# Token mixing gets the urgent rank, and the stacked keys' exponentials take the row maximum as ScalarE's bias

## The chip, the cores and the metric

One Trainium2 chip, one of its cores. The metric is the device time of one execution in microseconds; the median of three runs is given.

## The reference, cut to what matters

Two parts run one after the other: linear attention over 8 batches of 8 heads (576 tokens, 64 columns a head), and a mixer on its result.

```python
def phi(x):                                   # of queries and of keys
    proj = einsum('bhsd,df->bhsf', x, w_phi)  # 64 -> 128 features
    proj = proj - max(abs(proj), axis=-1, keepdims=True)
    return concatenate([exp(proj), exp(-proj)], axis=-1)
kv = einsum('bhsf,bhsd->bhfd', phi(k), v);  z = sum(phi(k), axis=2)
x = einsum('bhsf,bhfd->bhsd', phi(q), kv) / (einsum('bhsf,bhf->bhs', phi(q), z) + 1e-6)
x = x as (8, 576, 512)
h = relu(x^T @ w_tok1) @ w_tok2               # token mixing, 576 -> 256 -> 576
u = x + h^T
out = u + relu(u @ w_ch1) @ w_ch2             # channel mixing, 512 -> 1536 -> 512
```

Note the second exponential: it is exp(-(p - m)), that is exp(-p + m), where m is the largest absolute value of the row.

## The kernel before, in words

Attention works on pairs of heads, numbered i = 0 to 31, four pairs to a batch. `keys()` makes the features of the keys of a pair in five groups of up to two 128-token units and adds them to the pair's `pkv` sum on TensorE (`add_kv`, L326). `queries()` makes the features of the queries, turns them, splits them into a high and a low part (`turn`, L437 to L446) and multiplies them with the finished sum (`numerators`, `pn`); GpSimd's multiplication at L526 writes the attention result of a pair and segment into `xt`. Pairs 0 to 7 (batches 0 and 1) take a plain way; from pair 8 on, keys and queries are "stacked": a high and a low half of the input lie in one tile (`stack`, L215 and L216).

`less_max` is the helper that both share. For stacked inputs it multiplies with the projection (L241), copies one part out of PSUM on ScalarE (`part`, L248), adds on VectorE (`p`, L250, two buffers for keys and queries together), takes the row maximum of the absolute values on VectorE (`mx`, L255), and subtracts it on GpSimd (`pm`, L257). For plain inputs the subtraction runs on VectorE. `keys` then takes two exponentials on ScalarE (L301), one for each sign, over all units of the group.

`token_mix(b, h)` mixes the tokens of one half (two pairs) of batch b: per unit two transposes into `px` (L550), a split on ScalarE and VectorE into `xh` and `xl` (L566, in L77 and L80), matmuls into `pa`; then a ReLU into `ah` and `al` (L575, L576), matmuls into `ph`, and an addition into `xt` (L585). It issues no DMA. From batch 1 on its PSUM tiles `pa`, `px` and `ph` come from the pool REST, five rotating banks that it shares with the projections, `pkv`, `pt` and `pn` of attention. `channel_mix(i)` takes 256 tokens at a time, 18 chunks in all: copies `uh` and `ul`, then six up-projections `h` (24 matmuls each) that alternate with six down-projections `acc` (24 each); `h` has one bank, emptied by ScalarE (`gh`, L616) and VectorE (`gl`, L617). Chunk i starts once the batch of its last token is mixed.

All matmuls written through `mm3` carry line L86, so they are told apart by their tiles.

Two things set the order. `weave` calls the five streams in turn, by shares, and so fixes the order of the program text. Then the framework's planner orders each engine's queue by simulating the kernel: of the instructions that are ready it takes the one with the first rank. The rank is the place in the text, unless the stream is marked urgent (the third entry of its line in L694) and all weights are loaded in the text (L681): then an instruction is ranked as if it stood at the start of the program. Once a queue is ordered, each engine works it off strictly in that order.

Of the kernel before, what the change touches and what calls it, by code (L numbers as in the profile page):

```python
# [12 lines left out]
AF = mybir.ActivationFunctionType  # L13
ALU = mybir.AluOpType
# [5 lines left out]
NP = H // 2  # L20
# [27 lines left out]
def mixer_kernel(ctx, tc, qk, vm, vt, w_phi, w1, w2, wc1, wc2d, out):  # L48
    nc = tc.nc

    cst = ctx.enter_context(tc.tile_pool(name="cst", bufs=1))
    wk = ctx.enter_context(tc.tile_pool(name="wk", bufs=2))
# [17 lines left out]
    def column(pool, n, **kw):  # L70

        return pool.tile([P, 32], F32, **kw)[:, :n]
# [147 lines left out]
    def less_max(ts, units, name, base=None, early=False):  # L220

        n, kind = len(units), name[0]
        if early and base == D:
            ps = ps_a.tile([P, 2, 2, F], F32, tag=f"a{nplain['k'] % 2}", name=f"pp{name}")
            nplain["k"] += 1
        elif early and base == 0 and (nplain["q"] % 2 == 0 or nplain["q"] >= BORROWED):
            ps = ps_h.tile([P, 2, 2, F], F32, tag="h", name=f"pp{name}")
            nplain["q"] += 1  # L230
        elif early and base == 0:
            ps = ps_w.tile([P, 2, 2, F], F32, name=f"pp{name}", **REST)
            nplain["q"] += 1
        elif kind == "k":
            ps = ps_w.tile([P, 2, 2, F], F32, name=f"pp{name}", **REST)
        else:
            ps = ps_w.tile([P, 2, 2, F], F32, name=f"pp{name}", **REST)
        for i, u in enumerate(units):
            t, c = (ts[1], 512) if u is None else (ts[u[0]], P * u[1])
            if base is None:  # L240
                nc.tensor.matmul(ps[:, i].rearrange("p two f -> p (two f)"), t[:, c:c + P],  # L241
                                 wp2.rearrange("p two f -> p (two f)"), start=True, stop=True)
            else:
                rows = slice(D, P) if name == "k0_0" else slice(0, P)
                nc.tensor.matmul(ps[:, i, 0], t[rows, c:c + P], wz[rows, base // D], start=True, stop=True)  # L245
        if base is None:
            part = wk.tile([P, 2, F], F32, tag="part", name=f"part{name}")
            nc.scalar.copy(part[:, :n], ps[:, :n, 1])  # L248
            pr = wk.tile([P, 2, F], F32, tag="p", name=f"p{name}")
            nc.vector.tensor_tensor(pr[:, :n], ps[:, :n, 0], part[:, :n], op=ALU.add)  # L250
            pr, eng = pr[:, :n], nc.gpsimd
        else:
            pr, eng = ps[:, :n, 0], nc.vector
        mx = column(wk, 2, tag=f"mx{kind}", name=f"mx{name}")
        nc.vector.tensor_reduce(mx[:, :n], pr, axis=AX.X, op=ALU.max, apply_absolute_value=True)  # L255
        pm = wk.tile([P, 2, F], F32, tag=f"pm{kind}", name=f"pm{name}", bufs=1 if kind == "t" else 2)
        eng.tensor_tensor(pm[:, :n], pr, mx[:, :n].unsqueeze(2).to_broadcast([P, n, F]), op=ALU.subtract)  # L257
        return pm

    nplain = {"k": 0, "q": 0}  # L260
    raws, pairs, kvs, loaded = {}, {}, {}, set()
# [2 lines left out]
    def load(i):  # L264

        raw = wk.tile([P, 2 * S], F32, tag="raw", name=f"raw{i}", bufs=1)
        lo, hi = (D if i <= PLAIN else 0), (D if i == B * NP else P)
        nc.sync.dma_start(raw[lo:hi], qk[i, lo:hi])
        raws[i] = raw
# [12 lines left out]
    def keys():  # L282
        groups = [[(0, 0), (0, 1)], [(0, 2), (0, 3)], [(1, 0), (1, 1)], [(1, 2), (1, 3)], [None]]
        todo = None
        for i in range(B * NP):
            yield from until(lambda: i < 2 or i - 2 in asked)
            if i < PLAIN:
                load_plain(i)
            else:
                load(i)  # L290
            v_sb, queue = vtiles[i % 2], nc.sync if i else nc.scalar
            queue.dma_start(v_sb[:, 0:4].rearrange("p u j d -> p (u j) d")[:, :, :D], vm[i])
            for j in range(2):
                queue.dma_start(v_sb[j * D:(j + 1) * D, 4, j, :D], vt[i, j])
            plain = D if i < PLAIN else None
            ts = pairs[i] if i < PLAIN else stack(raws[i], D, f"k{i}")
            for g, us in enumerate(groups):
                pm = less_max(ts, us, f"k{i}_{g}", plain, i < NP)
                kp = wk.tile([P, 2, 2, F], F32, tag="kp", name=f"kp{i}_{g}")
                for sg in range(2):  # L300
                    nc.scalar.activation(kp[:, :len(us), sg], pm[:, :len(us)], AF.Exp, scale=1.0 - 2.0 * sg)  # L301
                yield 0.22
                if todo:
                    add_kv(*todo)
                    yield 0.82
                todo = (i, g, us, kp, v_sb)
        add_kv(*todo)
        yield 0.82
# [40 lines left out]
    def queries():  # L349
        waiting, split_up, row_major, pm = [], [], [], None  # L350
        pieces = [(i, k, j) for i in range(B * NP) for k in range(2) for j in range(2)]
        n = 0
        while n < len(pieces) or waiting or split_up or row_major:
            for done in row_major:
                flip(*done)
                yield 0.2
            row_major = []
            for work in split_up:
                yield from until(lambda: work[0] in kvs)
                if work[0] < ROWS:  # L360
                    row_major += [done for done in (row_numerators(*work),) if done]
                else:
                    numerators(*work)
                yield 0.75
            split_up = []
            while waiting and len(split_up) < 2 and (waiting[0][0] <= n or n >= len(pieces)):
                due, work = waiting.pop(0)
                split_up.append(turn(*work, pm if via(work[0]) and n < len(pieces) else None))
                yield 0.02 if via(work[0]) else 0.25
            if n < len(pieces):  # L370
                i, k, j = pieces[n]
                if (k, j) == (0, 0):
                    plain = 0 if i < PLAIN else None
                    if i < PLAIN:
                        yield from until(lambda: i in pairs)
                        ts = pairs[i]
                    else:
                        yield from until(lambda: i + 1 in raws or i + 1 == B * NP)
                        if i + 1 == B * NP:
                            load(i + 1)  # L380
                        ts = stack(raws[i + 1], 0, f"q{i}")
                    asked.add(i)
                    tail = less_max(ts, [None], f"t{i}", plain, i < NP)
                    yield 0.11
                pm = less_max(ts, [(j, 2 * k), (j, 2 * k + 1)], f"q{i}_{k}{j}", plain, i < NP)
                if via(i):
                    across(i, k, j, pm, tail)
                waiting.append((n + 1 + BEHIND * via(i), (i, k, j, pm, tail)))
                yield 0.22
            n += 1  # L390
# [3 lines left out]
    def via(i):  # L394
        return i >= ROWS and i % NP < TURNED
# [134 lines left out]
    def until(cond):  # L530
        while not cond():
            yield None
# [130 lines left out]
    def token_stream():  # L663
        for b in range(B):
            for h in range(2):
                yield from until(lambda: b * NP + 2 * h + 1 in attended and (b > 0 or NP - 1 in kvs))
                yield from token_mix(b, h, xts[b])
            mixed.add(b)
# [6 lines left out]
    def weave(streams):  # L675

        streams = [[g, share, urgent, 0.0] for g, share, urgent in streams]
        now = 0.0
        while streams:
            for s in sorted(streams, key=lambda s: s[3]) * 2:  # L680
                with tc.high_priority() if s[2] and NE - 1 in loaded else nullcontext():  # L681
                    step = next(s[0], "end")
                if step is None:
                    continue
                now = max(now, s[3])
                if step == "end":
                    streams.remove(s)
                else:
                    s[3] = max(s[3], now - LAG) + max(step, 0.01) / s[1]
                break  # L690
            else:
                raise RuntimeError("every stream waits")

    weave([(keys(), 5.2, True), (queries(), 5.2, True), (token_stream(), 8.0, False),  # L694
           (load_weights(), 10.0, False), (channel_stream(), 19.5, False)])


# [40 lines left out]
```

## Time and profile before

| | |
|---|---|
| median of 3 runs | 1117.81 us (1116.67 to 1118.49) |
| the profiled execution | 1116.6 us |
| its span, first to last instruction | 1114.7 us |
| TensorE busy | 1089.5 us, 98%, 9040 matmuls |
| VectorE busy | 721.1 us, 65% |
| GpSimd busy | 571.8 us, 51% |
| ScalarE busy | 560.9 us, 50% |
| mean granted TensorE clock | 0.995 |

The profile is of one execution. A matmul's end in it is modelled, and neighbouring matmuls overlap, so a TensorE that is busy all the time is not one at its peak: the number of matmuls in a stretch, held against a stretch where nothing interferes, says more than the busy share.

### The profile page before, as it was taken

To read this page: it belongs to the slowest core of one execution; us is meant where nothing else is said; L and a number is where in the kernel's file an instruction comes from. 1 tells how busy PE (TensorE), PEld (TensorE's weight loads), DVE (VectorE), ACT (ScalarE), POOL (GpSimd) and SP (SyncE) were. 2 spreads that over 40 slices of the span, in tenths; PEclk is the share of its full clock that TensorE was granted. 3 is DMA by queue.
4 is the path that set the end of the run, shared out by engine and by line. 5 is a ranking of instruction groups with operands and counts; after the bars stand their busy time and mean duration, and the time that the engine had idled before them with its cause. 6 is when DMAs were issued, how large, how long until landed. Compare 5 with 4: busy or idle time off the path is not lost.

```text
span 1114.7 us, 24745 instructions
## 1 busy us (share of the span) xinstructions
PE 1089.5 (98%) x9040; PEld 1074.3 (96%) x9040; DVE 721.1 (65%) x1775; ACT 560.9 (50%) x1589; POOL 571.8 (51%) x1043
## 2 busy tenths in 40 slices
PE   8998999999999899999999999999999999999998
PEld 7898999989999899999999999999999999999998
DVE  6889873557668775867676585774767687642111
ACT  5665542446546565665555464554555666541110
POOL 2235341467648674768667384664666776420110
PEclk9999999999999899999999999999999999999999
DMA  8454411133313332333233132141332323200000
GB/s 215 129 158 146 146 31 52 33 94 76 72 47 94 76 77 77 80 83 81 70 81 68 57 84 72 44 104 41 83 79 55 88 71 64 57 8 19 20 20 20
DMA packets 186746, 82.75 MB, mean 74 GB/s; under 512 B 159424, under 2 KB 171200, under 8 KB 186624
## 3 DMA queue, kind: packets, MB, share of 16 engines
q1 hardware_dynamic: 185104, 80.74, 27.9%
q8 instruction: 72, 1.18, 0.5%
q10 hardware_dynamic: 1520, 0.43, 0.2%
q14 instruction: 50, 0.41, 0.1%
HBM read 57.54 MB, written 23.59 MB: 73 GB/s over the span
## 4 chain that ended last, share of the span: by engine, by line
PE 83%; DVE 6%; POOL 5%; ACT 2%; issue 2%; DMA 2%; SPq 0%; ACTq 0%; POOLq 0%; DVEq 0%
PE h L86 25%; PE acc L86 24%; PE pkv L326 8%; PE pn L86 6%; PE ph L86 4%; PE pa L86 4%; PE pr L471 2%; PE ppk L241 2%; PE ppq L241 2%; POOL stq L216 1%; PE ppk L245 1%; PE px L550 1%; PE ppq L245 1%; POOL pmq L257 1%; PE pt L429 1%
## 5 line engine op out<-in xcount | busy, mean ns | idle before, releaser
L86 PE MATMUL acc<-gh,wc 128*128 128x256 f32 x1728 | 342.1, 284 | 1.8 <-ACT gh L616 1.6
L86 PEld LDWEIGHTS acc<-gh,wc 128*128 128x128 f32 x1728 | 275.4, 188 | 2.8 <-ACT gh L616 2.7
L86 PE MATMUL h<-uh,wc_h 128*128 128x256 f32 x864 | 245.3, 284 | 3.1 <-DVE gl L617 3.0
L86 PE MATMUL h<-uh,wc_l 128*128 128x256 f32 x864 | 244.4, 283 | 0.0
L86 PE MATMUL h<-ul,wc_h 128*128 128x256 f32 x864 | 243.0, 281 | 0.0
L86 PE MATMUL acc<-gl,wc 128*128 128x256 f32 x864 | 242.7, 283 | 0.0
L86 PEld LDWEIGHTS h<-uh,wc_h 128*128 128x128 f32 x864 | 162.7, 188 | 4.4 <-DVE gl L617 3.1
L326 PE MATMUL pkv<-v,kp 128*128 128x65 f32 (+2 forms) x1152 | 164.6, 269 | 1.2 <-ACT kp L301 1.1
L301 ACT ACTIVATE kp<-pmk 128x256 f32<-128x256 f32 (+1 forms) x320 | 109.4, 389 | 108.1 <-POOL pmk L257 82.8
L86 PEld LDWEIGHTS acc<-gl,wc 128*128 128x128 f32 x864 | 162.8, 188 | 0.3 <-DVE gl L617 0.2
L86 PEld LDWEIGHTS h<-ul,wc_h 128*128 128x128 f32 x864 | 162.7, 188 | 0.1
L86 PEld LDWEIGHTS h<-uh,wc_l 128*128 128x128 f32 x864 | 162.5, 188 | 0.1
L326 PEld LDWEIGHTS pkv<-v,kp 128*128 128x128 f32 x1152 | 153.5, 192 | 2.4 <-ACT kp L301 1.8
L617 DVE SCALAR_TENSOR_TENSOR gl<-h,gh 128x512 fp32r<-128x512 f32 x108 | 74.0, 685 | 123.7 <-ACT gh L616 120.7
L616 ACT ACTIVATE gh<-h 128x512 fp32r<-128x512 f32 x108 | 64.3, 596 | 119.4 <-PE h L86 117.8
L446 POOL TENSOR_TENSOR ql<-qf,qh 128x320 fp32r<-128x320 f32 (+1 forms) x96 | 80.1, 835 | 62.4 <-ACT qh L445 58.8
L597 POOL TENSOR_TENSOR ul<-xt,uh 128x64 fp32r<-128x64 f32 (+3 forms) x120 | 61.4, 537 | 87.6 <-ACT uh L596 86.9
L86 PE MATMUL pn<-qh,kv 128*128 128x320 f32 (+1 forms) x384 | 105.2, 304 | 0.9 <-ACT qh L445 0.6
L216 POOL TENSOR_TENSOR stk<-raw,stk 64x512 fp32r<-64x512 f32 (+1 forms) x48 | 68.5, 1428 | 66.6 <-DVE stk L215 45.3
L257 POOL TENSOR_TENSOR pmk<-pk,mxk 128x256 f32<-128x256 f32 (+1 forms) x120 | 71.7, 598 | 57.8 <-DVE mxk L255 56.9
L437 ACT ACTIVATE qf<-qt 128x320 f32<-128x320 f32 (+1 forms) x192 | 81.8, 436 | 37.4 <-POOL qf L436 36.5
L445 ACT ACTIVATE qh<-qt 128x320 fp32r<-128x320 f32 (+1 forms) x192 | 83.0, 437 | 31.4 <-POOL qh L444 25.8
(129 smaller groups left out, 2305.5 us busy)
## 6 DMA issues: line engine op xcount, KB each, us to landing
raw<-in_qk SPq DMA_DIRECT2D x23, 576.0 KB, 3.9
rawc<-in_wc SPq DMA_DIRECT2D x24, 512.0 KB, 4.3
v<-in_vm SPq DMA_DIRECT2D x31, 256.0 KB, 3.9
dq<-tq SPq DMA_DIRECT2D x24, 320.0 KB, 2.1
qt<-dq SPq DMA_DIRECT2D x96, 80.0 KB, 2.8
dq<-tq SPq DMA_DIRECT2D x24, 256.0 KB, 2.0
qt<-dq SPq DMA_DIRECT2D x96, 64.0 KB, 2.8
out_x<-xt SPq DMA_DIRECT2D x12, 256.0 KB, 2.1
```

The costliest lines, as they stand in the source:

```text
L86: nc.tensor.matmul(o, a, m, start=first and i == 0, stop=last and i == 2, skip_group_check=group_ok)
L216: nc.gpsimd.tensor_tensor(t[lo:lo + D], src, t[base:base + D].bitcast(F32), op=ALU.subtract)
L241: nc.tensor.matmul(ps[:, i].rearrange("p two f -> p (two f)"), t[:, c:c + P], wp2.rearrange("p two f -> p (two f)"), start=True, stop=True)
L257: eng.tensor_tensor(pm[:, :n], pr, mx[:, :n].unsqueeze(2).to_broadcast([P, n, F]), op=ALU.subtract)
L301: nc.scalar.activation(kp[:, :len(us), sg], pm[:, :len(us)], AF.Exp, scale=1.0 - 2.0 * sg)
L326: nc.tensor.matmul(o, kp[:, n, sg], v, start=g == 0 and n == 0 and sg == 0, stop=u is None, skip_group_check=True)
L437: nc.scalar.activation(full, src, AF.Exp, scale=1.0 - 2.0 * sg)
L445: nc.scalar.activation(hi, src, AF.Exp, scale=1.0 - 2.0 * sg)
L446: (nc.gpsimd if sg else nc.vector).tensor_tensor(lo, full, hi.bitcast(F32), op=ALU.subtract)
L597: nc.gpsimd.tensor_tensor(l[:, d:d + n], t[:, c, o:o + n], h[:, d:d + n].bitcast(F32), op=ALU.subtract)
L616: nc.scalar.activation(gh, ph, AF.Relu)
L617: nc.vector.scalar_tensor_tensor(gl, ph, 0.0, gh.bitcast(F32), op0=ALU.max, op1=ALU.subtract)
```

## The change

The token stream becomes urgent, like keys and queries. For stacked keys `less_max` no longer subtracts: it negates the maximum on VectorE into a new tile `nmx` (one buffer) and returns the projection with both columns; `keys` then takes each exponential unit by unit, with the negated maximum as bias for the positive sign and the maximum itself for the negative sign. Plain keys, and all queries, stay as they are. No DMA is added or moved in the text.

```diff
+        if base is None and kind == "k":
+            nmx = column(wk, 2, tag="nmx", bufs=1, name=f"nmx{name}")
+            nc.vector.tensor_scalar(nmx[:, :n], mx[:, :n], -1.0, None, op0=ALU.mult)
+            return pr, (nmx, mx)
         pm = wk.tile([P, 2, F], F32, tag=f"pm{kind}", name=f"pm{name}", bufs=1 if kind == "t" else 2)
         eng.tensor_tensor(pm[:, :n], pr, mx[:, :n].unsqueeze(2).to_broadcast([P, n, F]), op=ALU.subtract)
-        return pm
+        return (pm, None) if kind == "k" else pm
...
-                pm = less_max(ts, us, f"k{i}_{g}", plain, i < NP)
+                pm, mx = less_max(ts, us, f"k{i}_{g}", plain, i < NP)
                 kp = wk.tile([P, 2, 2, F], F32, tag="kp", name=f"kp{i}_{g}")
                 for sg in range(2):
-                    nc.scalar.activation(kp[:, :len(us), sg], pm[:, :len(us)], AF.Exp, scale=1.0 - 2.0 * sg)
+                    if mx is None:
+                        nc.scalar.activation(kp[:, :len(us), sg], pm[:, :len(us)], AF.Exp, scale=1.0 - 2.0 * sg)
+                        continue
+                    for u in range(len(us)):
+                        nc.scalar.activation(kp[:, u, sg], pm[:, u], AF.Exp, scale=1.0 - 2.0 * sg,
+                                             bias=mx[sg][:, u:u + 1])
...
-    weave([(keys(), 5.2, True), (queries(), 5.2, True), (token_stream(), 8.0, False),
+    weave([(keys(), 5.2, True), (queries(), 5.2, True), (token_stream(), 8.0, True),
            (load_weights(), 10.0, False), (channel_stream(), 19.5, False)])
```

## Rows read from the trace of the kernel before

**Rows 1.** The page: span, busy time of each engine, and the granted clock.

```profile
span 1114.7 us, 24745 instructions
...
PE 1089.5 (98%) x9040; PEld 1074.3 (96%) x9040; DVE 721.1 (65%) x1775; ACT 560.9 (50%) x1589; POOL 571.8 (51%) x1043
...
PEclk9999999999999899999999999999999999999999
```

**Rows 2.** Busy time by stretch: length, each engine (instructions), granted clock, DMA share, GB/s.

```profile
224.00:252.00 28.00, 25.11 (x201) 24.02 (x200) 17.19 (x43) 13.23 (x41) 18.10 (x34) 1.00 0.37 94
298.00:328.00 30.00, 29.43 (x244) 29.02 (x243) 16.23 (x41) 11.24 (x31) 8.75 (x18) 1.00 0.18 54
358.00:383.00 25.00, 20.54 (x125) 18.03 (x125) 17.31 (x47) 14.82 (x45) 14.98 (x32) 0.86 0.29 79
392.00:420.00 28.00, 28.00 (x239) 28.00 (x239) 20.80 (x52) 18.10 (x54) 20.45 (x41) 1.00 0.35 85
490.00:505.00 15.00, 14.15 (x112) 13.62 (x111) 11.71 (x33) 8.05 (x26) 8.53 (x19) 1.00 0.26 78
890.00:905.00 15.00, 14.17 (x113) 13.65 (x111) 12.01 (x33) 7.92 (x25) 9.08 (x18) 1.00 0.25 79
1036.00:1064.00 28.00, 28.00 (x240) 28.00 (x240) 4.97 (x9) 4.29 (x9) 2.86 (x4) 1.00 0.07 20
```

**Rows 3.** Groups of instructions on TensorE in 358 to 383 us, channel mixing's `h`.

```profile
L86 PE MATMUL h<-uh,wc_l 128*128 128x256 f32 x2 | 0.6, 321 | 0.0
...
L86 PE MATMUL h<-uh,wc_h 128*128 128x256 f32 x1 | 0.3, 281 | 0.0
```

**Rows 4.** Instructions of `pa` alone, by stretch: TensorE, weight loads, VectorE, ScalarE.

```profile
298.00:328.00 30.00, 4.26 (x28) 3.74 (x28) 0.69 (x1) 0.60 (x1) 1.00 0.18 54
...
490.00:505.00 15.00, 4.42 (x28) 3.82 (x28) 0.69 (x1) 0.60 (x1) 1.00 0.26 78
```

**Rows 5.** Instructions in order of time from 296 us, across engines: start, length, engine.

```profile
296.06 0.38 PE L550 MATMUL px<-ident,xt 128*128 128x128 f32 x2
...
299.19 0.28 PE L86 MATMUL pa<-xh,w_h 128*128 128x256 f32 x1
```

**Rows 6.** GpSimd in order of time: two neighbouring multiplications that write attention's result.

```profile
296.77 0.75 POOL L526 TENSOR_TENSOR xt<-xt,den 128x256 f32<-128x256 f32 x1
...
328.21 0.87 POOL L526 TENSOR_TENSOR xt<-xt,den 128x320 f32<-128x320 f32 x1 [1.62 <-DVE den L524]
```

**Rows 7.** TensorE's waits after 160 us: total us, times, longest.

```profile
PE ph L86 <- ACT ah L575: 2.9, 3, 1.5
PE h L86 <- DVE gl L617: 2.2, 3, 1.3
PE pa L560 <- DVE xs L555: 1.9, 2, 1.3
```

**Rows 8.** Groups of instructions by form: count, busy us, mean ns, idle before.

```profile
L301 ACT ACTIVATE kp<-pmk 128x256 f32<-128x256 f32 x256 | 93.3, 411 | 88.2 <-POOL pmk L257 71.1 <-DVE pmk L257 10.2 <-PE pkv L326 4.6
...
L257 POOL TENSOR_TENSOR pmk<-pk,mxk 128x256 f32<-128x256 f32 x96 | 62.0, 645 | 56.2 <-DVE mxk L255 55.9
...
L301 ACT ACTIVATE kp<-pmk 128x128 f32<-128x128 f32 x64 | 16.2, 302 | 19.9 <-POOL pmk L257 11.7 <-DVE pmk L257 4.8 <-PE pkv L326 1.7
...
L485 DVE TENSOR_SCALAR dn<-pr 128x4 f32<-128x4 f32 x16 | 2.5, 154 | 6.0 <-PE pr L471 6.0
```

**Rows 9.** The same view: the two instructions that empty the bank of an up-projection.

```profile
L617 DVE SCALAR_TENSOR_TENSOR gl<-h,gh 128x512 fp32r<-128x512 f32 x108 | 74.0, 685 | 123.7 <-ACT gh L616 120.7 <-POOL wc L80 2.1
...
L616 ACT ACTIVATE gh<-h 128x512 fp32r<-128x512 f32 x108 | 64.3, 596 | 119.4 <-PE h L86 117.8 <-PE acc L86 0.7 <-POOL wc L80 0.2
```

**Rows 10.** ScalarE in order of time, 395 to 411 us: two exponentials back to back, each form.

```profile
395.38 0.49 ACT L301 ACTIVATE kp<-pmk 128x128 f32<-128x128 f32 x2
...
405.20 0.72 ACT L301 ACTIVATE kp<-pmk 128x256 f32<-128x256 f32 x2 [0.21 <-POOL pmk L257]
```

**Rows 11.** Waits of SyncE's DMA queue: total us, times, longest.

```profile
SPq L648 <- DVE xt L647: 187.6, 32, 34.0
```

## The prediction

> **What bounds the kernel now.** I read the page first: TensorE is busy for 1089.5 of 1114.7 us, no other engine for more than 65%, and its clock is granted in full but for one slice of forty [rows 1]. The change neither adds nor removes a matmul, so it can only win or lose where TensorE falls behind its own pace. The second view is the table by stretch, read by number of matmuls. Where channel mixing runs alone, 240 matmuls go through in 28 us, 8.57 per us; the mixed stretch of 392 to 420 us keeps that pace with 239 [rows 2]. Against it four stretches fall behind: 224 to 252 us does 201 matmuls, 23.5 us of work, 4.5 us lost; 358 to 383 us does 125, 14.6 us of work, 10.4 us lost; 490 to 505 and 890 to 905 us do 112 and 113, 13.1 and 13.2 us of work, 1.9 and 1.8 us lost [rows 2]. That is 18.6 us, and the most that better order can give after the weights are in. A part isn't loss: matmuls of 320 columns take longer than those of 256, and the stretch of 298 to 328 us, without a real hole in it, already lags by 1.5 us (244 matmuls, 28.5 us of work in 30) [rows 2]. Taking some 0.9 us off for each of the four leaves about 15 us.
>
> Why these stretches? In 358 to 383 us TensorE runs five matmuls of `h` [rows 3], where 25 us of channel mixing alone would be 214 (25 x 8.57): the next chunk waits for the second half of its batch to be mixed. With no channel work to fill in, TensorE goes at the pace of one short chain (waits of up to 1.5 us for `ah` and 1.3 us for `xs` [rows 7]), and the granted clock falls to 0.86 of the stretch, between its two levels of 1.2 and 2.4 GHz [rows 2]. The others are the same thing on a smaller scale.
>
> What makes the half late? One half of token mixing has 28 matmuls of `pa`. Where channel mixing has nothing to do, in 490 to 505 us, they and what follows take 15 us; where it is in full swing, in 298 to 328 us, the same 28 take the whole 30 us [rows 4]. The order of time shows how: two transposes for `px` run at 296.06 us, and the `pa` matmuls of that moment start only at 299.19 us, behind a block of channel matmuls [rows 5]. Attention, though urgent, stands still meanwhile: GpSimd finishes one result at 296.77 us and begins the next at 328.21 us [rows 6], and it is busy for 8.75 us of these 30 against 20.45 of 28 in the stretch without token mixing [rows 2]. My reading is that the low rank of the token half holds back the urgent streams behind it, through the five banks of REST that both take from in turn. The trace shows the standstill and its length, not the bank.
>
> **The change part by part: the rank.** Token mixing issues no DMA, and its instructions on the four engines move ahead of channel mixing only. Each half should go from some 28 us towards 15, attention should stand still 13 us less each time, and the second half of batch 2, which the hole at 358 us waits for, has one such standstill just ahead of it (298 to 328 us). Is this enough? The hole's 10.4 us is less than 13, so it closes. The work moved forward is paid by channel mixing, which keeps a backlog in that time instead of running dry. The two holes of 1.9 and 1.8 us have many standstills ahead of them and close too, and the one in 224 to 252 us has the halves of batch 1 ahead of it; of the latter I count 3 of 4.5 us, since its first half may be held by attention itself. Gain: 10.4 + 3 + 1.9 + 1.8 - 3.6 for the wide matmuls = 13.5 us.
>
> Against that stand new waits. TensorE now takes token matmuls the moment that the planner thinks them ready, and its queue is strict, so where a copy comes late everything behind it waits. Today TensorE waits 2.9 us for `ah` and 1.9 us for `xs` in all, in five cases, mostly within the holes [rows 7]. The bounds: nothing, if the planner's times are right, as they nearly are for attention; and one wait of 0.7 us each for `xs` and `ah` in each of the 14 halves of batches 1 to 7, 20 us (0.7 is about the smaller of such waits: 2.9 less 1.5 in two, 1.9 less 1.3 in one [rows 7]). I take 2 us, nearer to the first, because there is channel work to put in between, which the holes lacked. The token steps are also moved past other work on the queues of ScalarE, VectorE and GpSimd. On SyncE's queue stand the channel outputs, for which it waits 187.6 us in all, up to 34.0 us [rows 11]; loads behind an output that now comes later can come late. These waits are long already, and the largest gaps lie where nothing urgent follows, so I count nothing; without that cover one late load would cost one standstill of attention, and TensorE only if channel mixing ran dry again.
>
> **The keys.** There are 24 stacked pairs, 96 groups of two units and 24 of one. GpSimd loses 96 subtractions of 645 ns, 62 us, and 24 shorter ones [rows 8]. VectorE gains 120 negations; the nearest row is a 128x4 operation of 154 ns [rows 8], so 18 us. ScalarE takes four exponentials of 128 columns where it took two of 256: by means 4 x 302 - 2 x 411 = 386 ns a group [rows 8], 37 us in all. Back to back, two short ones take 0.49 us and two long ones 0.72 [rows 10], so the lower bound is 2 x 0.49 - 0.72 = 0.26 us, 25 us in all. No row has a bias that is a column. If fetching it made a short one as dear as a long one, it would be 4 x 411 - 822 = 822 ns a group, 79 us. I take 37, since scale and bias are part of the same instruction either way. In return ScalarE's idle time behind that subtraction, 71.1 + 11.7 = 82.8 us [rows 8], is partly saved: the negation takes 154 ns where the subtraction took 645.
>
> None of the three is the bound, and what hides the extra 386 ns is this: the bank of `h` must be empty when the next up-projection starts, and in between lie 24 `acc` matmuls, 24/8.57 = 2.8 us. Emptying takes 596 + 685 ns = 1.28 us [rows 9], which leaves 1.5 us. TensorE waits only 2.2 us for `gl` in the whole run after 160 us [rows 7]. A key group ahead of `gh` uses 0.39 us more of the slack, which costs little: 1 us in all. With that cover gone it would cost TensorE 37 us, or 79 at the upper bound. The other new wait is VectorE's: `nmx` has one buffer, so the next negation waits until the first exponentials have read the last, with `p` and every later VectorE step behind it; 1.2 us of exponentials a group against 120 groups in 1114.7 us, one in 9 us on average and more often where attention is dense, makes that rare.
>
> On the price of a bias a page speaks against this change: the Trainium skill, "ScalarE: Activation LUTs", section "What ACT_TABLE_LOAD costs", says that each operand that points to a column adds about 93 ns to such an instruction. No row here shows it. By it a group would cost 4 x (302 + 93) - 822 = 758 ns more, an estimate near the upper bound; that is twice the 386 ns, and the sum below would lose another 1 us of its gain.
>
> **The sum.** 13.5 - 2 - 1 = 10.5 us off. The profiled execution took 1116.6 us, 1.9 us more than its span and 1.2 less than the median; on the median, 1117.8 - 10.5 gives 1107.3 us, as span about 1104.
>
> **The rivals.** *Attention sets the time (A).* The halves get faster, but the holes stay, because keys and queries, not tokens, are late: in the hole VectorE is busy for 17.3 of 25 us, as dense as anywhere [rows 2]. Against it speaks that attention stands still for 31 us just before [rows 6]. Time: between 1116 and 1119 us, the 3 us of new waits against what small gain there is. *It doesn't do what it says (N).* If the standstill comes from something else, as results waiting for `xt` to be written out, the rank changes little: the same time as in A. *The channel's bank comes late (S).* Token splits, key exponentials and attention all now stand ahead of `gh` and `gl` on two strict queues. It decides from 1.5 us of work ahead of them: one key group (4 x 0.302 = 1.2 us) and one more copy, at half to all of `gh`'s 0.6 us, are enough. Its place is the chunks that run beside attention, by the order of batches some 12 of the 18 (chunks 2 to 13), 72 up-projections. If one in three then waits for 1 us, that is 24 us: 1107 + 24 = 1131 us; one in six gives 1119. Against it: today the urgent streams already stand ahead of them, at a cost of 2.2 us [rows 7].
>
> **How the numbers follow.** Forecast 0.60, A and N together 0.18, S 0.22. The forecast's own range, from the bounds: 15 us gained and no new waits gives 1102, with the whole 18.6 us 1099; with 6 us of waits more 1113. A difference of 0.2%, 2.2 us, is about what can be told from no change. A and N fall mostly within it. Of S a small part still ends even. So faster 0.62, same 0.16, slower 0.22. The range for 8 in 10 reaches from 1099 to the middle of S, 1125 us.
>
> **What would show it.** Right: in the table by stretch, all stretches from 220 us on have about 8.5 matmuls per us and a full clock; the 28 `pa` of a half lie within some 15 us; attention's last multiplication comes earlier, and the stretch of channel mixing alone at the end is longer by that; the subtraction on GpSimd stays only for queries and `pmt`, and ScalarE's waits before `kp` shrink. Wrong: a stretch without `h` as long as before (A, N); waits of `h` for `gl` or of `pa` for `xh` and `xl` well over 10 us (S); short exponentials nearer to 400 than to 300 ns (the upper bound).

## The result, and the profile after

The changed kernel takes 1105.09 us, median of 4 runs (1103.36 to 1107.16), against 1117.24 us of the kernel before beside it: ratio 0.9891, 95% interval 0.9869 to 0.9912, so 1.1% faster. The forecast was 1107.3 us. The profiled execution has a span of 1104.4 us, 10.3 us less than before.

The head of the page of the changed kernel: span, and busy time of each engine.

```profile
span 1104.4 us, 24901 instructions
...
PE 1084.4 (98%) x9040; PEld 1072.5 (97%) x9040; DVE 743.2 (67%) x1895; ACT 614.9 (56%) x1781; POOL 501.6 (45%) x923
```

The work of TensorE is the same 9040 matmuls. ScalarE is busy for 54 us more than before, VectorE for 22 us more, GpSimd for 70 us less [rows 1]. Now the table by stretch of the changed kernel, the same stretches as in [rows 2]:

```profile
224.00:252.00 28.00, 28.00 (x237) 28.00 (x236) 16.33 (x43) 16.89 (x54) 14.63 (x30) 1.00 0.34 86
298.00:328.00 30.00, 28.72 (x239) 28.34 (x238) 23.43 (x66) 18.45 (x57) 16.99 (x36) 1.00 0.35 87
358.00:383.00 25.00, 23.10 (x177) 22.68 (x176) 13.64 (x36) 12.39 (x40) 11.38 (x24) 0.93 0.19 48
...
490.00:505.00 15.00, 14.87 (x124) 14.59 (x122) 13.05 (x30) 9.69 (x30) 9.41 (x18) 1.00 0.29 69
890.00:905.00 15.00, 14.93 (x124) 14.83 (x125) 14.09 (x33) 9.65 (x30) 11.18 (x22) 1.00 0.21 47
1036.00:1064.00 28.00, 28.00 (x240) 28.00 (x240) 3.75 (x6) 4.30 (x9) 2.86 (x4) 1.00 0.00 1
```

Read the number in the first bracket, TensorE's matmuls. The four stretches have filled up, not all of them wholly: 201 became 237, 125 became 177, 112 and 113 became 124 each. As the changed kernel is some 10 us ahead by the last two, their lowest place lies earlier:

```profile
480.00:495.00 15.00, 14.87 (x120) 14.59 (x119) 10.03 (x27) 6.80 (x21) 7.68 (x17) 1.00 0.25 77
```

120 matmuls are 14.0 us of work, 1.0 us lost where it was 1.9, so this hole is about half closed, and the one near 890 us too (120 from 881 to 896 us). 358 to 383 us lags most (214 would be full pace), with a granted clock of 0.93, and for a new reason that is told below. Where the 10.3 us came from shows in longer stretches. First the kernel before, then the changed one:

```profile
160.00:260.00 100.00, 97.11 (x813) 95.10 (x812) 52.37 (x136) 41.57 (x122) 43.90 (x70) 1.00 0.22 56
260.00:400.00 140.00, 134.97 (x1089) 132.01 (x1088) 100.74 (x253) 80.40 (x238) 93.96 (x179) 0.98 0.31 77
400.00:540.00 140.00, 139.13 (x1166) 138.29 (x1165) 102.47 (x255) 82.04 (x241) 96.62 (x188) 1.00 0.31 74
540.00:680.00 140.00, 139.38 (x1168) 138.57 (x1167) 96.81 (x233) 77.60 (x221) 86.69 (x161) 1.00 0.30 76
```

```profile
160.00:260.00 100.00, 99.68 (x837) 97.91 (x836) 59.83 (x162) 52.73 (x158) 42.08 (x69) 1.00 0.22 59
260.00:400.00 140.00, 136.80 (x1129) 135.68 (x1129) 105.98 (x276) 88.91 (x271) 79.42 (x153) 0.99 0.32 79
400.00:540.00 140.00, 139.81 (x1176) 139.35 (x1176) 107.66 (x278) 94.08 (x286) 81.40 (x162) 1.00 0.32 76
540.00:680.00 140.00, 140.00 (x1179) 140.00 (x1179) 105.34 (x269) 89.16 (x260) 77.41 (x145) 1.00 0.30 76
```

The changed kernel is ahead by 24, 40, 10 and 11 matmuls in these four. At 8.57 per us that is 2.8 + 4.7 + 1.2 + 1.3 = 10 us, three quarters of it before 400 us. The gain is time that TensorE lost before.

The halves got shorter by much less than was forecast. The 28 matmuls of `pa` lie within 15 us in each half that I looked at, but that is little news: [rows 4] counts 28 of them in a window of 30 us, and a narrower window shows that before they took no more than 17 us of it. The view is that of `pa` alone, first one stretch of the kernel before, then three of the changed one:

```profile
299.00:316.00 17.00, 4.26 (x28) 3.74 (x28) 0.00 (x0) 0.26 (x1) 1.00 0.23 69
```

```profile
284.00:299.00 15.00, 5.21 (x28) 4.03 (x28) 0.28 (x1) 0.60 (x1) 1.00 0.37 95
474.00:489.00 15.00, 5.32 (x28) 4.02 (x28) 0.69 (x1) 0.60 (x1) 1.00 0.32 77
596.00:611.00 15.00, 5.08 (x28) 3.94 (x28) 0.56 (x1) 0.60 (x1) 1.00 0.40 105
```

A whole half goes from its first `px` to its last `ph`. For the first half of batch 2 that is 296.06 us [rows 5] to 326.61 us before, 30.5 us; in the changed kernel it is 281.38 to 308.47 us, 27.1 us. The last `ph` before, then the first `px` and the last `ph` after:

```profile
326.25 0.36 PE L86 MATMUL ph<-w_h,al 128*128 128x256 f32 x1
```

```profile
281.38 0.38 PE L559 MATMUL px<-ident,xt 128*128 128x128 f32 x2
...
308.07 0.40 PE L86 MATMUL ph<-w_h,al 128*128 128x256 f32 x2
```

The other halves of batches 2 to 7 that ran beside channel mixing took 30 to 35 us before and take 26 to 32 us now (the last half of all left aside). A half that had TensorE nearly to itself in a hole got longer: the one at 487 us before took 17.5 us, and it takes 26 us now.

The keys' part, as groups by form (count, busy us, mean ns, idle before). The last row is the exponential of plain keys of the same size, which has no column as bias:

```profile
L309 ACT ACTIVATE kp<-pk,mxk 128x128 f32<-128x128 f32 x216 | 76.5, 394 | 74.6 <-DVE mxk L255 73.4 <-PE pkv L335 0.2
L309 ACT ACTIVATE kp<-pk,nmxk 128x128 f32<-128x128 f32 x216 | 76.0, 392 | 4.5 <-DVE nmxk L258 3.4 <-PE pkv L335 0.5
...
L258 DVE TENSOR_SCALAR nmxk<-mxk 128x2 f32<-128x2 f32 x96 | 24.1, 251 | 1.8 <-ACT kp L309 0.5
...
L306 ACT ACTIVATE kp<-pmk 128x128 f32<-128x128 f32 x16 | 4.1, 302 | 6.0 <-DVE pmk L261 3.7 <-DVE dn L495 1.3 <-PE pkv L335 1.0
```

A bias from a column costs 393 - 302 = 91 ns an instruction. And ScalarE still waits 73.4 us before these exponentials, now for the maximum, where it waited 82.8 us for the subtraction [rows 8]. The exponentials with the maximum itself run ahead of those with its negative, so nearly all of the waiting is for the reduction and 3.4 us for the negation.

### The profile page after: what moved, and what is told of

The parts are those of the page before. It is cut to its first block, busy times and chain, and to the rows that moved or that the text cites. A ratio compares the mean times of both kernels' runs of the same rounds, so it can differ in the third digit from the quotient of the medians.

```text
span 1104.4 us, 24901 instructions
## 1 busy us (share of the span) xinstructions
PE 1084.4 (98%) x9040; PEld 1072.5 (97%) x9040; DVE 743.2 (67%) x1895; ACT 614.9 (56%) x1781; POOL 501.6 (45%) x923
## 4 chain that ended last, share of the span: by engine, by line
PE 89%; DVE 4%; DMA 3%; ACT 2%; POOL 2%; issue 1%; SPq 0%; ACTq 0%; POOLq 0%; DVEq 0%
PE h L86 27%; PE acc L86 26%; PE pkv L335 9%; PE pn L86 7%; PE ph L86 5%; PE pa L86 4%; PE ppk L241 2%; PE pr L480 2%; PE ppq L241 2%; DMA raw<-in_w 1%; PE px L559 1%; PE ppk L245 1%; PE ppq L245 1%; PE pa L569 1%; PE pt L438 1%
## 5 line engine op out<-in xcount | busy, mean ns | idle before, releaser
L335 PE MATMUL pkv<-v,kp 128*128 128x65 f32 (+2 forms) x1152 | 159.4, 269 | 1.3 <-ACT kp L306 0.7
L335 PEld LDWEIGHTS pkv<-v,kp 128*128 128x128 f32 x1152 | 149.5, 191 | 2.2 <-ACT kp L306 0.9
L309 ACT ACTIVATE kp<-pk,mxk 128x128 f32<-128x128 f32 x216 | 76.5, 394 | 74.6 <-DVE mxk L255 73.4
L216 POOL TENSOR_TENSOR stq<-raw,stq 64x512 fp32r<-64x512 f32 (+1 forms) x48 | 68.9, 1436 | 48.6 <-DVE stq L215 42.4
```

Of the source, the lines that this page charges most:

```text
L216: nc.gpsimd.tensor_tensor(t[lo:lo + D], src, t[base:base + D].bitcast(F32), op=ALU.subtract)
L309: nc.scalar.activation(kp[:, u, sg], pm[:, u], AF.Exp, scale=1.0 - 2.0 * sg, bias=mx[sg][:, u:u + 1])
L335: nc.tensor.matmul(o, kp[:, n, sg], v, start=g == 0 and n == 0 and sg == 0, stop=u is None, skip_group_check=True)
```

## The experiments

All times are medians, beside runs of the kernel before on the same chip, whose own median lies between 1117.2 and 1119.4 us.

**The two parts by themselves.** `rank_only` is the kernel before with one line changed, `keys_only` the changed kernel with that line taken back.

```diff
-    weave([(keys(), 5.2, True), (queries(), 5.2, True), (token_stream(), 8.0, False),
+    weave([(keys(), 5.2, True), (queries(), 5.2, True), (token_stream(), 8.0, True),
```

> The kernel before with the token stream urgent, and nothing else. Theory T (the rank brings the whole gain, by closing the stretches without channel work; the keys' part costs nothing and gives nothing): 10 to 14 us faster than before, 1104 to 1108 us, within 3 us of the changed kernel. Rival K (the keys' part brings a good share, because GpSimd's subtraction held attention up): 3 to 7 us faster than before, and the keys alone make up the rest. Rival C (the keys' part costs, since a bias from a column makes a short exponential 392 ns): 14 to 17 us faster, better than the changed kernel by 3 us or more.

> The changed kernel with the token stream not urgent: only the keys' exponentials with a bias. T: within 3 us of the kernel before, 1115 to 1120 us; the hole near 360 us stays, with fewer than 150 matmuls in its 25 us. K: 4 us faster or more. C: 3 us slower or more, with waits of h for gl over 5 us.

The rank alone: 1105.49 us, ratio 0.9881 (0.9846 to 0.9915), the same as the whole change. The keys alone: 1117.49 us, ratio 0.9995 (0.9981 to 1.0010), no change. T holds, K and C fall: the rank brings all of it, and 54 us more on ScalarE against 70 us less on GpSimd come out even. The table by stretch of the keys alone has the holes where they were:

```profile
224.00:252.00 28.00, 26.06 (x213) 25.25 (x211) 18.55 (x52) 16.65 (x52) 17.17 (x30) 1.00 0.38 93
358.00:383.00 25.00, 20.30 (x145) 17.70 (x144) 21.01 (x57) 17.02 (x52) 14.52 (x29) 1.00 0.30 81
490.00:505.00 15.00, 13.95 (x110) 13.40 (x109) 11.61 (x34) 10.36 (x32) 7.99 (x17) 1.00 0.26 82
```

They are a little shallower at the first two (213 and 145 matmuls for 201 and 125 [rows 2]), but the time doesn't show it. With the rank alone the hole near 360 us is closed outright:

```profile
358.00:383.00 25.00, 25.00 (x211) 25.00 (x210) 18.70 (x45) 14.54 (x45) 15.75 (x33) 1.00 0.26 71
```

In exchange that run does 66 matmuls in 252 to 264 us, 4.3 us lost, around a wait of the kind that the section on the late rank shows.

**Which halves.** The token stream is urgent only early, only late, or only in one batch; nothing else differs from the kernel before. The edit shown is the early one; the others ask for at least 3 mixed batches, for exactly 1, or for exactly 2.

```diff
-                with tc.high_priority() if s[2] and NE - 1 in loaded else nullcontext():
+                with tc.high_priority() if (len(mixed) < 3 if s[2] is None else s[2]) and NE - 1 in loaded else nullcontext():
...
-    weave([(keys(), 5.2, True), (queries(), 5.2, True), (token_stream(), 8.0, False),
+    weave([(keys(), 5.2, True), (queries(), 5.2, True), (token_stream(), 8.0, None),
```

> The kernel before with the token stream urgent only until batch 2 is mixed, later as before. T in its narrow form (the gain is the holes at 224 to 252 and 358 to 383 us, 3 + 10.4 us of the count in the prediction): 9 to 13 us faster than before. Rival W (the gain is spread over all batches, through less friction at every half): 3 to 6 us faster, for 4 of 14 halves.

> The kernel before with the token stream urgent only from batch 3 on. T in its narrow form: 1 to 4 us faster than before (the holes at 490 and 890 us, 1.9 and 1.8 us), and the hole near 360 us stays as it was, about 125 matmuls in 25 us. W: 7 to 10 us faster.

> The kernel before with the token stream urgent only for batch 1 (both halves). If each hole is closed by the standstill just ahead of it, as the prediction has it: 3 to 5 us faster, the hole at 224 to 252 us closed, the one near 360 us still there. Rival L (a lead gained early is kept, so the first standstill pays for the later holes too): 9 to 13 us faster, all of the gain, the hole near 360 us closed as well.

> The kernel before with the token stream urgent only for batch 2. By the prediction: 8 to 11 us faster, the hole near 360 us closed, the one at 236 to 245 us as before. Rival L, or a hole that attention itself sets: 0 to 4 us faster.

Urgent early: 1104.70 us, ratio 0.9882 (0.9844 to 0.9919), all of the gain from 4 of 14 halves. The late holes are still there in that run, 13 us earlier than before and as deep (112 and 113 matmuls before [rows 2]):

```profile
477.00:492.00 15.00, 14.15 (x112) 13.65 (x112) 11.75 (x32) 7.80 (x25) 8.28 (x17) 1.00 0.28 82
877.00:892.00 15.00, 14.17 (x112) 13.64 (x111) 12.02 (x33) 7.79 (x25) 9.09 (x17) 1.00 0.25 79
```

Urgent late: 1120.60 us, ratio 1.0025 (1.0007 to 1.0044), a loss of 2.8 us where T expected a gain and W a large one. Batch 1 alone: ratio 0.9939 (0.9916 to 0.9962), 6.8 us. Batch 2 alone: ratio 0.9927 (0.9902 to 0.9951), 8.2 us. W falls. The two batches add up to 15 us where together they give 13.2, so within these intervals the holes are nearly separate accounts, as the prediction had them. The stretch from 358 to 383 us, first with batch 1 urgent, then with batch 2:

```profile
358.00:383.00 25.00, 21.88 (x162) 19.77 (x161) 20.65 (x55) 15.39 (x47) 17.20 (x33) 1.00 0.34 92
```

```profile
358.00:383.00 25.00, 23.11 (x183) 22.23 (x184) 19.76 (x49) 12.71 (x38) 15.17 (x30) 1.00 0.35 85
```

Batch 1 alone takes this hole from 125 to 162 matmuls, so a lead gained early is partly kept: L holds in part. The gain of batch 1, 6.8 us, is above the 3 to 5 that I expected of its own hole, but its interval, 4.3 to 9.4 us, reaches into them. The standstill just ahead of this hole, 31.4 us before [rows 6], is 35.0 us long with batch 1 urgent and 24.5 us with batch 2, so its length alone doesn't fill the hole.

**What the rank costs late.** Urgent late closes the holes at 490 and 890 us (126 matmuls in 15 us each), and yet it loses. Its trace in order of time on ScalarE, then two stretches of it:

```profile
900.80 0.73 ACT L301 ACTIVATE kp<-pmk 128x256 f32<-128x256 f32 x2
907.42 0.65 ACT L518 COPY xt<-pn 64x320 f32<-64x320 f32 x2 [5.89 <-DMA out_x<-xt]
```

```profile
490.00:505.00 15.00, 15.00 (x126) 15.00 (x124) 9.71 (x23) 6.98 (x21) 8.52 (x21) 1.00 0.16 47
904.00:912.00 8.00, 6.06 (x38) 5.62 (x37) 4.00 (x12) 2.59 (x7) 1.36 (x2) 0.82 0.37 90
```

Attention is so early that its first result of a batch wants the `xt` tile of two batches before, whose output has not left yet: SyncE issues it at 904.08 us, in the middle of the wait. The copy waits 5.89 us at the head of ScalarE's queue, and everything else stands behind it. TensorE first misses the bank of the `pn` that this copy and VectorE's step after it (L519) empty:

```profile
908.45 0.50 PE L241 MATMUL ppq<-wp,stq 128*128 128x256 f32 x2 [1.70 <-DVE den L519]
```

It does 38 matmuls in 8 us, and after these 1.70 us without work its clock falls. The length of such a wait is not its price. The longest of this run, 6.29 us, ends at 785.69 us, and TensorE, which then waits only 0.24 us for the same bank, loses 1.0 us around it (111 matmuls in 14 us), with its clock granted in full; around the one of 5.89 us it loses 3.8 us:

```profile
779.00:793.00 14.00, 13.53 (x111) 12.92 (x110) 8.04 (x18) 4.05 (x13) 5.52 (x12) 1.00 0.17 54
900.00:914.00 14.00, 12.06 (x87) 11.62 (x87) 7.98 (x21) 4.42 (x12) 4.88 (x11) 0.88 0.28 62
```

(The expectation of `late_out` calls the dear one the longest; it isn't.) The kernel before has one such wait too, of 4.49 us, at 783.40 us. Two things could be at work in the late rank's loss, this wait or the other order alone. In the next four runs VectorE adds the channel result into a tile of the `g` tag, and the output leaves from there, so that `xt` is free without a landing. This changes nothing in what is computed.

```diff
+            y = streamed(wk, [P, 2, CH], F32, tag="g", name=f"y{i}_{k}", bufs=4)
             for b, t, o, n, s in segs:
                 v = t[:, 2 * k:2 * k + 2, o:o + n]
-                nc.vector.tensor_tensor(v, acc[k][:, :, d:d + n], v, op=ALU.add)
-                nc.sync.dma_start(out[b, :, 2 * k:2 * k + 2, s:s + n], v)
+                nc.vector.tensor_tensor(y[:, :, d:d + n], acc[k][:, :, d:d + n], v, op=ALU.add)
+                nc.sync.dma_start(out[b, :, 2 * k:2 * k + 2, s:s + n], y[:, :, d:d + n])
```

> The kernel before with the token stream urgent, and the channel result added into a tile of its own (of the tag that gh and gl rotate in) instead of into xt, so that xt comes free with VectorE's addition and not with the landing of the output DMA. Theory D (what the rank costs in the later batches is ScalarE's wait, at the head of its queue, for the output two batches back: 14.0 us in 5 waits in the run with the rank alone): those waits fall under 3 us, and it is 1 to 4 us faster than the run with the rank alone, 1101 to 1104 us. Rival G (the bank of gh and gl that waits for the output DMA now holds up the next chunk): same or slower, waits of h for gl or of gh for a DMA of over 5 us. Rival O (the later rank costs through order alone): waits gone, time the same within 1 us.

> Urgent only until batch 2 is mixed, together with the tile of its own for the channel result. By D it adds little to the run that is urgent early, where these waits are 1.6 us: within 2 us of it, 1102 to 1106 us. By G: slower by 3 us or more.

> Urgent only from batch 3 on, with the tile of its own for the channel result. Urgent late alone was 2.8 us slower than before, although it closes the holes at 490 and 890 us; its trace has 14.9 us of ScalarE waiting for an output DMA, and after the longest of these waits TensorE does 38 matmuls in 8 us. Theory D (this wait is what the late rank costs): 2 to 5 us faster than that run, so 1 to 3 us faster than before. Rival O (order alone): still 1 to 4 us slower than before.

> The changed kernel (rank and keys) with the tile of its own for the channel result. By D: 1 to 5 us faster than the changed kernel, 1100 to 1104 us. If the keys' part is neutral on top of the rank: within 2 us of the run with rank and tile but without the keys' part (1103.6 us). If the 54 us that it adds on ScalarE begin to count: 3 us slower than that run or more.

The clear case is `late_out`: 1113.47 us, ratio 0.9963 (0.9945 to 0.9981), against 1.0025 (1.0007 to 1.0044) without the tile, so 6.9 us gained, more than D expected. Its waits of ScalarE have no entry for an output DMA any more, and the same stretch runs at full pace, while the early holes, which it doesn't touch, are as before:

```profile
358.00:383.00 25.00, 19.56 (x128) 17.34 (x128) 17.91 (x49) 15.34 (x46) 14.63 (x31) 0.93 0.31 84
...
904.00:912.00 8.00, 8.00 (x71) 8.00 (x70) 6.83 (x14) 4.53 (x15) 6.05 (x14) 1.00 0.01 2
```

So the late rank's cost goes with this wait, and O falls there. What the tile does without the rank was not run, so a gain of its own within the 6.9 us isn't ruled out. With the rank on throughout, the tile takes those waits from 14.0 us to none, but the time is 1103.61 us, ratio 0.9874 (0.9846 to 0.9902), which can't be told from 0.9881 without it, so O stands there as well as D. With the whole change and the tile it is 1105.40 us, ratio 0.9881 (0.9865 to 0.9898), the same as without the tile: there D's gain is missing, and the keys' part is again neutral within the 2 us expected. Early rank with the tile is 1106.79 us, just above the 1102 to 1106 expected, ratio 0.9901 (0.9870 to 0.9932), not distinguishable from 0.9882. No version is clear of the changed kernel.

**How far ScalarE's cover reaches.** Every exponential of a stacked key is taken twice.

```diff
-                    for u in range(len(us)):
+                    for u in list(range(len(us))) * 2:
```

> The changed kernel with every exponential of a stacked key taken twice, the second over the first: 432 more instructions of about 393 ns, 133 us more on ScalarE back to back or 170 by means, 1.2 to 1.6 us more in one burst. It asks how far the cover of the bank of h reaches. Theory (what hides a key group is the 1.5 us of slack, and there is more elsewhere because the planner places the work): 0 to 6 us slower than the changed kernel. Rival S of the prediction (the channel's bank comes late once over 1.5 us stand ahead of its copies): 20 us slower or more, with waits of h for gl of over 10 us in all.

1113.67 us, ratio 0.9963 (0.9944 to 0.9982), so 8.6 us slower than the changed kernel (8 us by the two ratios) for 116 us more on ScalarE (730.7 us busy). It lies between the two expectations, and for a reason that neither named. TensorE's waits for `gl`, where S has its place, hardly grow:

```profile
PE h L86 <- DVE gl L626: 3.1, 5, 0.9
```

against those of the changed kernel:

```profile
PE h L86 <- DVE gl L626: 1.9, 4, 1.1
```

Instead the holes come back, here in the table by stretch:

```profile
358.00:383.00 25.00, 22.62 (x169) 20.54 (x168) 20.28 (x56) 19.95 (x64) 13.45 (x28) 1.00 0.36 91
483.00:502.00 19.00, 16.92 (x125) 15.18 (x124) 15.88 (x45) 15.23 (x50) 9.05 (x20) 1.00 0.39 101
```

125 matmuls in 19 us are 14.6 us of work, 4.4 us lost. ScalarE's extra time isn't paid at the bank of `h`; it makes attention late (its last result begins at 990.3 us, in the changed kernel at 979.6), and channel mixing runs dry again.

**What holds attention back.** Token mixing gets two banks of its own, REST has three.

```diff
-    REST = dict(tag="rest", bufs=5)
+    REST = dict(tag="rest", bufs=3)
...
-        return ps_w.tile(shape, F32, name=name, **REST)
+        return ps_w.tile(shape, F32, name=name, tag="tok", bufs=2)
```

> The kernel before, token stream not urgent, but from batch 1 on its PSUM tiles come from two banks of their own, and REST has three instead of five. Not a candidate, only a look at the standstill. If attention stands still because it takes REST banks in turn with token mixing of low rank: GpSimd's multiplications into xt go on while a half is mixed, no gap over 20 us at the halves. If the standstill has another cause: the gap of about 31 us (296.8 to 328.2 us before) and those like it stay. The time itself can be worse, as three banks slow attention and two slow the tokens: 1110 to 1160 us.

1250.96 us in one run, well above the 1110 to 1160 expected. The longest gaps between GpSimd's results are some 22 to 27 us there, against 31 us before, but gaps of 16 to 18 us lie everywhere between them: three banks slow attention as a whole, and two slow the tokens. By the sign that I had set, no gap over 20 us, the reading fails; but with everything slower the sign is a poor one. The run shows that banks are scarce (132 us for this division of the same five) and doesn't tell whether the standstill before came from taking them in turn. The trace before adds that attention doesn't stop in it: from 298 to 328 us TensorE runs 12 of its `pn` matmuls, between steps of the half, and only GpSimd's result is missing.

```profile
298.00:328.00 30.00, 2.08 (x12) 1.78 (x12) 1.20 (x3) 0.99 (x3) 1.00 0.18 54
```

## Why the prediction held

*The holes are the prize*: right. The count from [rows 2] was 18.6 us at most and 13.5 us recoverable, 10.5 after new waits; the interval of the ratio stands for 9.8 to 14.6 us, and the matmul counts place about 10 us in these stretches. Urgent early alone gives the same with the late holes still there, so the place of the gain is shown, not only argued. Urgent late alone gives nothing, and with the tile about 4 us; so the late holes are worth something too, which without the tile the wait for `xt` takes back.

*Which standstill closes which hole*: nearly right. Batch 2 alone gave 8.2 us against the 10.4 that I gave to the hole near 360 us, batch 1 alone 6.8 us against 3. The first was too large because batch 1 carries part of it.

*A half from 28 to 15 us, and 13 us less of standstill each time*: wrong in size, and here luck helped. The prediction took the window of [rows 4] for the length of the `pa` matmuls, and a half alone in a hole for what the rank would make of one beside channel mixing. The half measured went from 30.5 to 27.1 us. The standstill ahead of the hole near 360 us, 31.4 us between two results [rows 6], shrank by 10 us in the changed kernel (289.61 to 310.77 us, 21 us) and by 5 us with the rank alone (291.44 to 317.72 us, 26 us). So the test that was to show that the hole closes, 13 us against 10.4, would have failed with the measured numbers, and yet with the rank alone it closes. In that run attention is already 5 us ahead where the standstill starts, and it is with batch 1 alone urgent too. The gain came out because it was counted from the matmuls lost and not from the length of a half. Nor are all standstills shorter. Before, six gaps between two results are longer than 25 us; now two are, of 32 us from 347 us on and of 52 us from 728 us on. The first ends with the wait for `xt` shown below. The second stays without that wait: in the run with the rank and the tile it is 58.6 us, so its cause is open.

*Through the banks of REST*: left open.

*New waits, 2 us*: too small, and the kind was wrong. I looked for waits of TensorE for `xh`, `xs` and `ah`; those on `ah` and `xs` after 160 us fell from 4.8 us [rows 7] to none in the list. What came instead is the wait for `xt`, which I had named only under N, as something that might make the rank useless. In the changed kernel it makes the remaining hole:

```profile
367.67 0.40 ACT L454 ACTIVATE qh<-qt 128x256 fp32r<-128x256 f32 x1
374.11 0.65 ACT L527 COPY xt<-pn 64x320 f32<-64x320 f32 x2 [6.04 <-DMA out_x<-xt]
```

```profile
366.00:380.00 14.00, 12.10 (x87) 11.68 (x87) 7.99 (x23) 5.68 (x18) 4.65 (x11) 0.88 0.28 62
```

87 matmuls in 14 us are 10.2 us of work, 3.8 us lost. It stands at the same place as the old hole but has another cause.

*The keys cost 1 us*: right in sum, since the part alone changes nothing that can be told from 1 us. Two of its terms were mis-sized. Each exponential takes 393 ns, not 302, so the four cost 750 ns more than the two they replace, near my upper bound of 822 ns and not at the 386 that I took; ScalarE's busy time grew by 54 us and not by 37. The reason given, that scale and bias belong to the same instruction either way, fell. The Trainium skill ("ScalarE: Activation LUTs", section "What ACT_TABLE_LOAD costs") gives about 93 ns for a column as operand, and the trace agrees with 91. The negation takes 251 ns by mean, not 154, though its median, 158 ns, is near; VectorE is busy for 22 us more in all against 18. And ScalarE's waiting before the exponentials was to shrink; it only changed what it waits for.

*The longer tail of channel mixing alone*: wrong. Attention's last result begins at 979.6 us in place of 990.0, 10.4 us earlier, and the span ends 10.3 us earlier, so the tail is as long as it was, about 125 us. Attention doesn't keep a lead: just before the gap of 52 us its results are 23 us ahead of the kernel before, just behind it 9 us. That it waits for channel mixing to be done with the `xt` tile of two batches before would explain this, but no run shows it.

*The rivals*: A and N fall with the holes. S didn't occur, and doubling the exponentials shows that its place was wrong: more ScalarE work is felt through attention's pace first.

## What to carry to other kernels

Where one engine is the bound and still has holes, count its instructions in each stretch against a stretch that runs undisturbed: the difference is the whole prize, and its place tells which stream was late. A consumer that runs dry is helped by ranking the producer's slow last step ahead of the holes. Ranked higher behind them as well, it gained nothing more here and met the next limit, a tile not yet written out, where the waiting copy stops a whole queue. Read how long a step takes from its first and last instruction: a window that holds all of it gives only an upper bound. Test a change of two parts by its parts: one here was all, the other nothing.

## What was new about the hardware

A column as bias made a 128x128 exponential 393 ns instead of 302 in the same run. In the run with the late rank the granted clock, after 1.70 us in which TensorE waited for one bank, read 0.82 for 904 to 912 us, a mix of its two levels of 1.2 and 2.4 GHz, and TensorE lost 3.6 us there (38 matmuls in 8 us). Around ScalarE's wait of 6.04 us in the changed kernel the clock read 0.88 for 14 us, and 3.8 us were lost. A wait of 6.29 us on ScalarE at another place of the first run, where TensorE waited 0.24 us for that bank, left the clock at 1.00 and cost 1.0 us.
